# A slot of the load ring traded for a kept key tile, with projections done head by head, in a two-layer decode kernel

## Chip, cores, metric

One core of one Trainium2 chip. The metric is the device time of the kernel in microseconds (us), median of the runs of one kernel.

Names in this text: PE, DVE, ACT, POOL and SP are engines of the core. In this kernel PE does matmuls and transposes; DVE, ACT and POOL do the rest of the arithmetic and copy results; SP issues the loads. The DMA moves data from HBM, the large memory, into the core's own memory, where the kernel's tiles lie in 128 partitions; PE writes its results to PSUM. PE's "granted clock" is the share of full speed that the profile says it had. A load is "under way" from its issue by SP until all of it has landed. A run counts as slow when it is over 1.5% above the fastest run of its kernel.

Ratios and intervals are computed as the mean time of one kernel's fast runs over that of the other kernel's fast runs of the same rounds, so they are not quite the ratio of the medians that are quoted. Where a difference in us against the kernel before is given for an experiment ("-40 us"), it is the difference of the means of all fast runs of the two kernels in that set of runs.

## The reference, cut to what matters

```python
# B = 8 sequences, one new token each, D = 448, 16 query heads, 8 key/value heads,
# 4096 cached keys of 256 numbers (bf16); MLP width 1792
x = x + attention(layernorm(x), k_cache, v_cache, wq, wo)
y = layernorm(x)                        # with one token the block's mixer adds only zeros (w1, w2 drop out)
x = x + y + gelu(layernorm(y) @ w3) @ w4
# then both once more: a second layer with the SAME caches and weights
```

Both layers read the same key and value caches (134 MB each). A pass over keys and values for each layer would load all of it twice. The kernel keeps some transposed keys on the chip between the layers, so that layer 1 does not load and transpose them again.

## The kernel before

There are 8 batch elements, 8 key/value heads and 2 layers, so 128 "heads" of work in a fixed order `seq`. For each head, keys come in two half tiles of 1 MiB (2048 keys), values in two. All loads go through one ring of slots in this order; a slot is reused when PE has read it.

```python
N_RING = 5          # slots of 1 MiB (8 KB of each partition)
N_KEEP = 9          # kept half tiles of transposed keys, also 8 KB of each partition
CHAIN = 60
...
ring = [sb(f"ring{i}", [P, HALF, DH], bf) for i in range(N_RING)]
keep = [nc.alloc_sbuf_tensor(f"keep{i}", [P, HALF, P], f32) for i in range(N_KEEP)]
...
def kept(h, a):                       # half tile a of head h is kept for layer 1
    k = 2 * h + a
    return k if k < N_KEEP else None

def streamed(layer, h, a):            # is it loaded?
    return layer == 0 or kept(h, a) is None
...
def load_next():                      # the next chunk of the fixed order, into slot n % N_RING
    ...
    t, r = ring[n % N_RING]
    op("sp", lambda e: e.dma_start(t[:, :, :], src[b, h]...), writes=[r], dma=...)
```

One head of attention: PE transposes the keys in eight groups of four 128x128 blocks (`turn`), DVE or ACT copies each group from PSUM to SBUF, PE multiplies them with the queries (`score`), DVE/POOL/ACT make the softmax, and PE multiplies with the values of the head before (`pv`).

```python
ON_ACT = (1, 3, 5, 7)                 # of the eight groups of a head, those that ACT copies; DVE has the others
...
stream = any(streamed(layer, h, a) for a in range(2))
turns(0)
if stream and g > 1: finish(g - 2)
scores(0)
if stream: pv(g - 1, 0)
elif g > 1: finish(g - 2)
turns(1)
scores(1)
softmax(g)
if not stream: pv(g - 1, 0)           # a kept head frees two value slots one right after the other
pv(g - 1, 1)
```

Between the layers each batch element needs a **chain**: output projection, residual, norm, w3, GELU, w4, norm, query projection. The chain is a Python generator; `pump()`, called 14 times in a streamed head, puts its next steps into the instruction streams, as fast as a credit allows (a step with matmuls costs 1.0, one without 0.4). Before the first layer-1 head of the element, what is left of the chain is put in at once (`drain`).

```python
def mix(lo, n, then_q, project_out=True):
    for c in range(KC):
        for t in range(0, 32, 8):
            outputs(lo, n, c, range(t, t + 8), t == 0, True)      # 16 groups of 8 matmuls
            yield
    ...                                                           # norm, w3 (6 groups), gelu, w4 (8), norm
    yield from queries(lo, n)                                     # 16 groups, then one copy per half of the queries

def pump():
    credit["n"] = min(1.0, credit["n"] + credit["rate"]) if jobs else 0.0   # rate = CHAIN / (14*(per-1)) = 1.01
    while credit["n"] > 0.0:
        credit["n"] -= step()
...
if layer == 1 and all(s_[:2] != (1, b) for s_ in seq[:g]):
    drain()
```

In the order of heads, "kept" phases of ten heads (five layer-1 heads whose keys are kept, alternating with five layer-0 heads of the next element) alternate with "free" phases of five or six fully streamed heads. The chains run in the free phases.

Of the kernel before, what the change touches and what calls it, by code (L numbers as in the profile page):

```python
# [3 lines left out]
P = 128  # L4
B = 8
D = 448
HQ = 16
HKV = 8
# [10 lines left out]
GELU_K = 0.7978845608028654  # L19
RSQRT_MAGIC = 0x5F3759DF  # L20

N_RING = 5
N_KTR = 4
N_TK = 4
N_KEEP = 9
N_REP = 24
N_MLP = 24
CHAIN = 60
N_PS = 2


# [97 lines left out]
def decode_two_layers(nc, A_x, A_k_cache, A_v_cache, A_wq, A_wo, B_w3, B_w4, out):  # L129
# [42 lines left out]
    hw, r_hw = sb("hw", [P, NF, B], f32)  # L172
    hT, r_hT = sb("hT", [P, NF, B], bf)
    qT = nc.alloc_sbuf_tensor("qT", [P, B, 2, HQ], bf)
    r_q = [Res() for _ in range(B)]
    oT = nc.alloc_sbuf_tensor("oT", [P, HQ, 2, B], bf)
    r_o = [Res() for _ in range(B)]
    pT = [sb(f"pT{i}", [P, NI, 2], bf) for i in range(N_PS)]
# [15 lines left out]
    C_H = 32  # L194
    C_Q = 160
    C_L = 480


    op("pool", lambda e: e.memset(ident[:, :], 0.0), writes=[r_ident])
# [8 lines left out]
    op("dve", lambda e: e.memset(lnT[:, :, :], 0.0), writes=[r_ln, r_lift])  # L208

    op("dve", lambda e: e.memset(mm[64:P, C_Y:C_Y + B], 0.0), writes=[r_mm])  # L210


    full = N_KEEP // 2
# [155 lines left out]
    def kr(kc):  # L369
        return P if kc > 0 else 64  # L370
# [28 lines left out]
    def project(cols, r_w, at, ts, upper, n):  # L399

        def f(e):
            last = None
            for t in ts:
                for kc in (1, 2, 3, 0):
                    rhs = lnT[:, KC if kc == 0 and upper else kc, 0:n]
                    last = e.matmul(room(P, at + t * B, n), cols(kc, t), copies(rhs, n),  # L406
                                    start=(kc == 1), stop=(kc == 0), skip_group_check=True)
            return last
        op("pe", f, reads=r_w + [r_ln] + ([r_lift] if upper else []), writes=[r_mm])

    def queries(lo, n):

        yield from layernorm(lo, n, False)
        scaled(lnT, r_ln, 0, n)
        yield
        yield
        for t in range(0, 32, 2):
            project(wq_cols, wq_r, C_Q, range(t, t + 2), t >= 16, n)
            if t == 0:
                lift(n)  # L420
            yield
        for c in range(2):
            op("dve", lambda e, c=c: e.tensor_copy(  # L423
                qT[:, lo:lo + n, c, :],
                mm[:, C_Q:C_Q + 32 * B].rearrange("p (a c n) -> p n c a", n=B, c=2)[:, 0:n, c, :]),
               reads=[r_mm], writes=[r_q[b] for b in range(lo, lo + n)])

    def outputs(lo, n, c, ts, first, alone):

        def f(e):  # L430
            w = kr(c)
            last = None
            for t in ts:
                at = C_Y + c * B + lo
                cols = oT[:, t // 2, t % 2, lo:lo + n]
                last = e.matmul(room(w, at, n) if alone else mm[0:w, at:at + n], wo[:, t, row0(c):row0(c) + w],  # L436
                                copies(cols, n) if alone else cols, start=first and t == ts[0],
                                stop=False, skip_group_check=True)
            return last
        op("pe", f, reads=[r_wo] + [r_o[b] for b in range(lo, lo + n)], writes=[r_mm])  # L440

    def mix(lo, n, then_q, project_out=True):

        y_ = mm[:, C_Y:C_Y + KC * B].rearrange("p (c n) -> p c n", n=B)[:, :, lo:lo + n]
        x_ = xT[:, :, lo:lo + n]
        if project_out:
            for c in range(KC):
                for t in range(0, 32, 8):
                    outputs(lo, n, c, range(t, t + 8), t == 0, True)
                    yield  # L450
        op("dve", lambda e: e.tensor_tensor(x_, y_, x_, ALU.add), reads=[r_mm, r_x], writes=[r_x])
        yield from layernorm(lo, n, True)
        scaled(lnT, r_ln, 1, n)

# [23 lines left out]
           reads=[r_hb, r_hw], writes=[r_hT])  # L478
        yield
        for c in range(KC):  # L480
            for half in range(2):
                def f(e, c=c, half=half):
                    w = kr(c)
                    last = None
                    for t in range(7 * half, 7 * half + 7):
                        last = e.matmul(room(w, C_Y + c * B + lo, n), w4[:, t, row0(c):row0(c) + w],  # L486
                                        copies(hT[:, t, 0:n], n), start=(t == 0), stop=(t == NF - 1), skip_group_check=True)
                    return last
                op("pe", f, reads=[r_w4, r_hT], writes=[r_mm])
                yield  # L490
        op("dve", lambda e: e.scalar_tensor_tensor(x_, y_, 0.5, xres[:, :, 0:n], ALU.mult, ALU.add),
           reads=[r_mm, r_xres], writes=[r_x])
        yield
        if then_q:
            yield from queries(lo, n)

    jobs = []

    credit = {"n": 0.0, "rate": 1.0}

    def step():

        if jobs:
            n = len(S.ops["pe"])
            try:
                next(jobs[0])
            except StopIteration:
                jobs.pop(0)
            return 1.0 if len(S.ops["pe"]) > n else 0.4
        return 1.0  # L510

    def pump():
        credit["n"] = min(1.0, credit["n"] + credit["rate"]) if jobs else 0.0
        while credit["n"] > 0.0:
            credit["n"] -= step()

    def drain():
        while jobs:
            step()


# [26 lines left out]
    def attend(g):  # L548
# [41 lines left out]
        def score(f):  # L590
            kt, r_kt = kts[f]

            def fn(e):
                last = None
                for i in range(4):
                    at = C_S + 2 * (4 * f + i)
                    for c in range(2):

                        last = e.matmul(pst[:, at:at + 2 * N_REP].rearrange("p (r j) -> p r j", j=2), kt(i, c),  # L599
                                        repeated(qT[:, b, c, 2 * h:2 * h + 2]), start=(c == 0),  # L600
                                        stop=(c == 1), skip_group_check=True)
                return last
            op("pe", fn, reads=[r_kt, r_q[b]], writes=[r_ps])

        def turns(a):
            for f in range(4 * a, 4 * a + 4):
# [98 lines left out]
    for g, (layer, b, h) in enumerate(seq):  # L705
        last_of[layer, b] = g

    def all_but(h):

        ts = [t for t in range(32) if t // 4 != h]  # L710
        for c in (1, 2, 3, 0):
            for n in range(0, 28, 14):
                outputs(B - 1, 1, c, ts[n:n + 14], c == 1 and n == 0, False)
                yield

    def after(g):

        layer, b, h = seq[g]
        if g == len(seq) - 2:
            jobs.append(all_but(seq[-1][2]))  # L720
        if last_of[layer, b] != g:
            return
        if layer == 0:
            credit["rate"] = CHAIN / (14 * (per - 1))
            jobs.append(mix(b, 1, True))
        elif b == B - 2:
            jobs.append(mix(0, B - 1, False))
        elif b == B - 1:
            for c in range(KC):
                outputs(B - 1, 1, c, range(4 * h, 4 * h + 4), False, False)  # L730
            jobs.append(mix(B - 1, 1, False, False))

    jobs.append(queries(0, B))
    for g, (layer, b, h) in enumerate(seq):
        if layer == 1 and all(s_[:2] != (1, b) for s_ in seq[:g]):
            drain()
        w = attend(g)
        if g == 0:
            next(w)
            drain()  # L740
        for _ in w:
            pass
        if late:
            late.pop(0)()
# [76 lines left out]
```

## Time and profile before

| | before |
|---|---|
| time, median of 2 runs | 1261.01 us (1260.38 to 1261.63) |
| HBM read | 471.93 MB |
| DMA queue busy | 93.5% of 16 engines' span |
| PE busy | 77% |
| mean granted clock of PE | 0.885 |

The page of the kernel before: the rate in 40 equal slices of 31.6 us, and the loads' queue.

```profile
GB/s 316 378 415 420 374 322 398 420 404 295 384 419 419 371 335 421 419 419 355 358 421 419 378 307 418 421 419 308 399 420 420 401 319 421 420 414 295 362 312 122
...
q1 hardware_dynamic: 70496, 471.97, 93.5%
...
HBM read 471.93 MB, written 0.01 MB: 374 GB/s over the span
```

Rates of 419 to 421 GB/s are the best that occur, and they occur in many slices; about every 145 us a slice falls to 295 to 360. The part of the page on loads gives size and median time from issue to landing:

```profile
ring<-in_A_v_cache_dram SPq DMA_DIRECT2D x256, 1024.0 KB, 10.1
ring<-in_A_k_cache_dram SPq DMA_DIRECT2D x184, 1024.0 KB, 10.3
```

A load takes 2.5 us at 420 GB/s but 10 us from issue to landing: some four loads are under way at once.

Two stretches of the same trace (columns: from:to in us, their length, busy us and instructions of PE, of its weight loads, DVE, ACT and POOL, then PE's granted clock, mean DMA busy share, GB/s). The first is a kept phase, the second a chain:

```profile
340.00:400.00 60.00, 46.40 (x843) 40.89 (x840) 21.39 (x63) 15.83 (x46) 5.27 (x14) 0.89 1.01 420
700.00:747.00 47.00, 39.05 (x800) 34.64 (x800) 21.69 (x91) 10.91 (x29) 3.41 (x9) 0.85 0.90 341
```

In the first the DMA is the limit: 420 GB/s. In the second it moved 341 GB/s. What PE waited for, over the whole run (total us, number of waits, longest):

```profile
PE tk L575 <- DMA ring<-in_A_k_cache_dram: 124.1, 82, 2.7
...
PE mm L406 <- DVE lnT L365: 42.9, 10, 11.6
...
PE mm L406 <- DVE t L365: 31.3, 9, 5.0
...
PE mm L486 <- DVE hT L477: 10.1, 10, 1.5
```

L575 is a transpose of keys, L406 a projection (w3 or queries) and L486 one with w4; `lnT` and `t` are the two last DVE steps of a norm. The chain at 700 us shows what such a wait is (PE's instructions in time order: start, us, what, times; in brackets the idle time before and what ended it):

```profile
710.08 1.59 PE L575 MATMUL tk<-ident,ring 128*128 128x128 f32 x12 [0.15 <-DMA ring<-in_A_k_cache_dram]
714.89 0.26 PE L406 MATMUL mm<-lnT,w_sb 128*128 128x24 bf16 x3 [3.22 <-DVE t L365]
...
715.35 1.11 PE L575 MATMUL tk<-ident,ring 128*128 128x128 f32 x4
```

PE stands 3.22 us until the norm is done. Before the wait 12 transposes took 1.59 us, after it four take 1.11 us: half speed. The Trainium skill, page "TensorE: Matmul & The Clock Gate", Part 1, says PE's clock halves after an idle window of about 3.4 us and comes back after about as long a busy one; this trace agrees in kind (here a wait of 3.22 us was enough, and transposes were slow until about 720.8 us, some 6 us, with PE not busy all of that time).

### The profile page before, as it was taken

What the parts mean: (1) busy time and instruction counts of PE and PEld (TensorE: products, weight loads), DVE (VectorE), ACT (ScalarE), POOL (GpSimd) and SP (SyncE); (2) the same over time, 40 slices, a digit from 0 to 9 for tenths busy, and PEclk for the clock granted to TensorE, in tenths of its full rate; (3) what the DMA queues carried; (4) which work ended last, traced back from release to release, by engine and by line L of the source; (5) the groups of instructions that cost most, each with busy time, mean ns of one, the idle gap of its engine ahead of it and who ended that gap; (6) DMA issues with size and microseconds to landing.
All of it is one profiled execution on the core that took longest, in us unless ns stands there. A gap on an engine that the chain in (4) does not pass through costs nothing.

```text
span 1262.4 us, 42152 instructions
## 1 busy us (share of the span) xinstructions
PE 975.7 (77%) x19067; PEld 857.2 (68%) x19067; DVE 483.6 (38%) x1691; ACT 314.7 (25%) x891; POOL 104.9 (8%) x281
## 2 busy tenths in 40 slices
PE   2777887787886887877887888787777887787885
PEld 2666776676775776776776777676666776676774
DVE  2323442335333443335333443344333443334243
ACT  1223222222222222222222222231222222222120
POOL 0000000000000010000000000000100000000100
PEclk7879888888989989898889888897988988998886
DMA  8999989998999989999999989998999989998982
GB/s 316 378 415 420 374 322 398 420 404 295 384 419 419 371 335 421 419 419 355 358 421 419 378 307 418 421 419 308 399 420 420 401 319 421 420 414 295 362 312 122
DMA packets 70675, 474.66 MB, mean 376 GB/s; under 512 B 7248, under 2 KB 13280, under 8 KB 13792
## 3 DMA queue, kind: packets, MB, share of 16 engines
q1 hardware_dynamic: 70496, 471.97, 93.5%
q8 instruction: 149, 2.44, 0.8%
q14 instruction: 30, 0.25, 0.0%
HBM read 471.93 MB, written 0.01 MB: 374 GB/s over the span
## 4 chain that ended last, share of the span: by engine, by line
PE 44%; DMA 41%; DVE 9%; issue 4%; POOL 1%; SPq 1%; ACT 0%; POOLq 0%; ACTq 0%
DMA ring<-in_A_k_cache_dram 39%; PE tk L575 20%; PE ps L599 9%; PE pvb L673 5%; PE mm L406 4%; PE mm L436 2%; DMA ring<-in_A_v_cache_dram 2%; PE pvb L691 2%; DVE ktr L582 2%; PE mm L486 1%; SPq L269 1%; DVE sm L326 1%; DVE sm L327 1%; DVE sm L344 1%; DVE sm L325 1%
## 5 line engine op out<-in xcount | busy, mean ns | idle before, releaser
L575 PE MATMUL tk<-ident,ring 128*128 128x128 f32 x2944 | 459.3, 309 | 124.9 <-DMA ring<-in_A_k_cache_dram 124.1
L575 PEld LDWEIGHTS tk<-ident,ring 128*128 128x128 f32 x2944 | 370.1, 158 | 163.8 <-DMA ring<-in_A_k_cache_dram 153.5
L582 DVE COPY ktr<-tk 128x512 f32<-128x512 f32 x224 | 154.6, 690 | 244.8 <-PE tk L575 244.3
L580 ACT COPY ktr<-tk 128x512 f32<-128x512 f32 x224 | 131.2, 586 | 404.4 <-PE tk L575 404.4
L673 PE MATMUL pvb<-ring,pT 128*2 128x256 bf16 x4096 | 161.6, 279 | 47.8 <-DMA ring<-in_A_v_cache_dram 42.0
L582 DVE COPY keep<-tk 128x512 f32<-128x512 f32 x144 | 99.5, 691 | 170.2 <-PE tk L575 169.6
L599 PE MATMUL ps<-qT,keep 128*128 128x48 bf16 x4608 | 157.0, 187 | 5.6 <-DVE qT L423 3.6
L599 PEld LDWEIGHTS ps<-qT,keep 128*128 128x128 bf16 x4608 | 148.3, 99 | 17.7 <-issue 7.7
L580 ACT COPY keep<-tk 128x512 f32<-128x512 f32 x144 | 84.3, 586 | 266.3 <-PE tk L575 266.3
L655 ACT ACTIVATE pT<-ps,nb 128x32 bf16<-128x32 f32 x256 | 76.4, 298 | 252.3 <-DVE nb L651 234.7
L599 PE MATMUL ps<-qT,ktr 128*128 128x48 bf16 x3584 | 135.4, 188 | 0.6
L599 PEld LDWEIGHTS ps<-qT,ktr 128*128 128x128 bf16 x3584 | 122.5, 100 | 6.7 <-ACT ktr L580 1.5
L673 PEld LDWEIGHTS pvb<-ring,pT 128*2 128x2 bf16 x4096 | 76.0, 82 | 74.1 <-DMA ring<-in_A_v_cache_dram 47.3
L649 POOL PARTITION_ALL_REDUCE gm<-pm x128 | 45.4, 355 | 861.3 <-DVE pm L646 861.3
L406 PE MATMUL mm<-lnT,wq_sb 128*128 128x24 bf16 x864 | 48.0, 184 | 40.6 <-DVE lnT L365 40.3
L406 PEld LDWEIGHTS mm<-lnT,wq_sb 128*128 128x128 bf16 x864 | 43.3, 102 | 48.5 <-DVE lnT L365 42.4
L679 DVE COPY ob<-pvb 128x256 f32<-128x256 f32 x128 | 53.7, 420 | 51.1 <-PE pvb L673 50.5
L646 DVE TENSOR_REDUCE pm<-ps 128x2 f32<-128x64 f32 x128 | 28.7, 224 | 113.0 <-PE ps L599 113.0
L436 PE MATMUL mm<-oT,wo_sb 128*128 128x24 bf16 (+5 forms) x1280 | 61.5, 184 | 3.4 <-issue 2.2
L660 POOL PARTITION_ALL_REDUCE dn<-rs x128 | 51.1, 399 | 150.6 <-ACT pT L655 150.6
L691 PE MATMUL pvb<-ident,ob 128*128 128x128 f32 x256 | 58.4, 314 | 6.1 <-DVE ob L679 6.1
L436 PEld LDWEIGHTS mm<-oT,wo_sb 128*128 128x128 bf16 (+1 forms) x1280 | 52.1, 104 | 13.9 <-issue 10.1
(65 smaller groups left out, 477.4 us busy)
## 6 DMA issues: line engine op xcount, KB each, us to landing
ring<-in_A_v_cache_dram SPq DMA_DIRECT2D x256, 1024.0 KB, 10.1
ring<-in_A_k_cache_dram SPq DMA_DIRECT2D x184, 1024.0 KB, 10.3
wo_sb<-in_A_wo_dram SPq DMA_DIRECT2D x1, 3584.0 KB, 15.2
wq_sb<-in_A_wq_dram SPq DMA_DIRECT2D x3, 1024.0 KB, 11.2
w_sb<-in_B_w_dram SPq DMA_DIRECT2D x1, 1568.0 KB, 18.5
w_sb<-in_B_w_dram SPq DMA_DIRECT2D x3, 448.0 KB, 14.9
wqf_sb<-in_A_wq_dram SPq DMA_DIRECT2D x2, 256.0 KB, 14.8
w3f_sb<-in_B_w_dram SPq DMA_DIRECT2D x2, 112.0 KB, 15.8
```

The lines of the kernel that those rows point to most:

```text
L406: last = e.matmul(room(P, at + t * B, n), cols(kc, t), copies(rhs, n), start=(kc == 1), stop=(kc == 0), skip_group_check=True)
L436: last = e.matmul(room(w, at, n) if alone else mm[0:w, at:at + n], wo[:, t, row0(c):row0(c) + w], copies(cols, n) if alone else cols, star ...
L575: last = e.transpose(bank[:, j * P:(j + 1) * P], src[:, 4 * (f % 4) + j, :].bitcast(f32), ident4[:, :])
L580: op("act", lambda e: e.copy(flat, bank[:, :]), reads=[r_bank], writes=[r_kt])
L582: op("dve", lambda e: e.tensor_copy(flat, bank[:, :]), reads=[r_bank], writes=[r_kt])
L599: last = e.matmul(pst[:, at:at + 2 * N_REP].rearrange("p (r j) -> p r j", j=2), kt(i, c), repeated(qT[:, b, c, 2 * h:2 * h + 2]), start=(c ...
L649: op("pool", lambda e: e.partition_all_reduce(gm[q][0][:, :], pm[q][0][:, :], P, ReduceOp.max), reads=[pm[q][1]], writes=[gm[q][1]])
L655: return e.activation(pT[q][0][:, :, :].rearrange("p i j -> p j i")[:, j, :], pst[:, C_S:C_S + 2 * NI].rearrange("p (i j) -> p j i", j=2)[ ...
L660: op("pool", lambda e: e.partition_all_reduce(dn[q][0][:, :], rs[q][0][:, :], P, ReduceOp.add), reads=[rs[q][1]], writes=[dn[q][1]])
L673: last = e.matmul(pvb[at:at + 2, 0:DH], pT[q][0][:, a * HALF + i, :], v[:, i, :], start=(a == 0 and i < 4), stop=(a == 1 and i >= HALF - 4 ...
L679: op("dve", lambda e: e.tensor_copy(ob[:, :], pvb[:, 0:DH]), reads=[r_pv], writes=[r_ob])
L691: last = e.transpose(pvb[:, DH + c * P:DH + (c + 1) * P], ob[:, c * P:(c + 1) * P], ident4[:, :])
```

## The change

The intent: a fifth slot of the ring and a tenth kept half tile cost the same memory (8 KB of each partition). Trade the slot for the tile: eight loads of 1 MiB less. With that, the chain is lightened: the output projection of a head is done as soon as the head is done, the queries become usable head by head, and the chain runs at a slower pace of 0.6 step per pump.

```diff
-N_RING = 5
+N_RING = 4
-N_KEEP = 9
+N_KEEP = 10
-CHAIN = 60
+RATE = 0.6
@@ queries
+        for h in range(HKV):
+            for t in (4 * h, 4 * h + 2):
+                project(wq_cols, wq_r, C_Q, range(t, t + 2), t >= 16, n)
+                ...
+            op("dve", ... copy of this head's queries ..., reads=[r_mm], writes=[r_q[lo][h]])
+            ready[lo] = h + 1
+            yield
@@ output projection
+    def output(b, h):                 # 16 matmuls of one head, then xT += on DVE; a "side" job that goes first
+        ...
-        if project_out:               # no longer the first 16 groups of the chain
-            for c in range(KC): ...
@@ w4: one group of 14 matmuls for each c, not two of 7
@@ the end: outputs of the last element per head too, instead of 112 matmuls held for the end
@@ main loop
-        if layer == 1 and all(s_[:2] != (1, b) for s_ in seq[:g]):
-            drain()
+        while layer == 1 and ready[b] <= h:
+            step()
```

(The order of heads and loads is the same, except for the eight loads that fall away.)

More of the change, by code (lines that the diff above doesn't have):

```diff
@@ L174, in decode_two_layers @@
     qT = nc.alloc_sbuf_tensor("qT", [P, B, 2, HQ], bf)
-    r_q = [Res() for _ in range(B)]
+    r_q = [[Res() for _ in range(HKV)] for _ in range(B)]
     oT = nc.alloc_sbuf_tensor("oT", [P, HQ, 2, B], bf)
@@ L196, in decode_two_layers @@
     C_L = 480
+    C_P = 448
     op("pool", lambda e: e.memset(ident[:, :], 0.0), writes=[r_ident])
@@ L210, in decode_two_layers @@
     op("dve", lambda e: e.memset(mm[64:P, C_Y:C_Y + B], 0.0), writes=[r_mm])
+    op("dve", lambda e: e.memset(mm[64:P, C_P:C_P + 1], 0.0), writes=[r_mm])
     full = N_KEEP // 2
@@ L416, in queries @@
         yield
-        for t in range(0, 32, 2):
-            project(wq_cols, wq_r, C_Q, range(t, t + 2), t >= 16, n)
-            if t == 0:
-                lift(n)
+        for h in range(HKV):
+            for t in (4 * h, 4 * h + 2):
+                project(wq_cols, wq_r, C_Q, range(t, t + 2), t >= 16, n)
+                if t == 0:
+                    lift(n)
+                yield
+            if n > 1:
+                continue
+            op("dve", lambda e, h=h: e.tensor_copy(
+                qT[:, lo, :, 2 * h:2 * h + 2],
+                mm[:, C_Q + 4 * h * B:C_Q + 4 * (h + 1) * B].rearrange("p (a c n) -> p n c a", n=B, c=2)[:, 0, :, :]),
+               reads=[r_mm], writes=[r_q[lo][h]])
+            ready[lo] = h + 1
@@ L421, in queries @@
             yield
         for c in range(2):
-            op("dve", lambda e, c=c: e.tensor_copy(
-                qT[:, lo:lo + n, c, :],
-                mm[:, C_Q:C_Q + 32 * B].rearrange("p (a c n) -> p n c a", n=B, c=2)[:, 0:n, c, :]),
-               reads=[r_mm], writes=[r_q[b] for b in range(lo, lo + n)])
-    def outputs(lo, n, c, ts, first, alone):
+            if n > 1:
+                op("dve", lambda e, c=c: e.tensor_copy(
+                    qT[:, lo:lo + n, c, :],
+                    mm[:, C_Q:C_Q + 32 * B].rearrange("p (a c n) -> p n c a", n=B, c=2)[:, 0:n, c, :]),
+                   reads=[r_mm], writes=[r for b in range(lo, lo + n) for r in r_q[b]])
@@ L430, in f @@
+    def output(b, h):
         def f(e):
-            w = kr(c)
             last = None
-            for t in ts:
-                at = C_Y + c * B + lo
-                cols = oT[:, t // 2, t % 2, lo:lo + n]
-                last = e.matmul(room(w, at, n) if alone else mm[0:w, at:at + n], wo[:, t, row0(c):row0(c) + w],
-                                copies(cols, n) if alone else cols, start=first and t == ts[0],
-                                stop=False, skip_group_check=True)
-            return last
@@ L440, in outputs @@
-        op("pe", f, reads=[r_wo] + [r_o[b] for b in range(lo, lo + n)], writes=[r_mm])
-    def mix(lo, n, then_q, project_out=True):
+            for c in range(KC):
+                w = kr(c)
+                for t in range(4 * h, 4 * h + 4):
+                    last = e.matmul(room(w, C_P + c, 1), wo[:, t, row0(c):row0(c) + w],
+                                    copies(oT[:, t // 2, t % 2, b:b + 1], 1), start=(t == 4 * h),
+                                    stop=(t == 4 * h + 3), skip_group_check=True)
@@ new lines, in f, with outputs @@
+            return last
+        op("pe", f, reads=[r_wo, r_o[b]], writes=[r_mm])
+        yield
+        op("dve", lambda e: e.tensor_tensor(xT[:, :, b], mm[:, C_P:C_P + KC], xT[:, :, b], ALU.add),
+           reads=[r_mm, r_x], writes=[r_x])
+    def outputs(lo, n):
+        for c in range(KC):
+            def f(e, c=c):
+                w = kr(c)
+                last = None
+                for t in range(32):
+                    last = e.matmul(room(w, C_Y + c * B + lo, n), wo[:, t, row0(c):row0(c) + w],
+                                    copies(oT[:, t // 2, t % 2, lo:lo + n], n), start=(t == 0),
+                                    stop=(t == 31), skip_group_check=True)
+                return last
+            op("pe", f, reads=[r_wo] + [r_o[b] for b in range(lo, lo + n)], writes=[r_mm])
+            yield
+        y_ = mm[:, C_Y:C_Y + KC * B].rearrange("p (c n) -> p c n", n=B)[:, :, lo:lo + n]
+        op("dve", lambda e: e.tensor_tensor(xT[:, :, lo:lo + n], y_, xT[:, :, lo:lo + n], ALU.add),
+           reads=[r_mm, r_x], writes=[r_x])
@@ L444, in mix @@
+    def mix(lo, n):
         y_ = mm[:, C_Y:C_Y + KC * B].rearrange("p (c n) -> p c n", n=B)[:, :, lo:lo + n]
         x_ = xT[:, :, lo:lo + n]
-        if project_out:
-            for c in range(KC):
-                for t in range(0, 32, 8):
-                    outputs(lo, n, c, range(t, t + 8), t == 0, True)
-                    yield
-        op("dve", lambda e: e.tensor_tensor(x_, y_, x_, ALU.add), reads=[r_mm, r_x], writes=[r_x])
         yield from layernorm(lo, n, True)
@@ L480, in mix, with f @@
         for c in range(KC):
-            for half in range(2):
-                def f(e, c=c, half=half):
-                    w = kr(c)
-                    last = None
-                    for t in range(7 * half, 7 * half + 7):
-                        last = e.matmul(room(w, C_Y + c * B + lo, n), w4[:, t, row0(c):row0(c) + w],
-                                        copies(hT[:, t, 0:n], n), start=(t == 0), stop=(t == NF - 1), skip_group_check=True)
-                    return last
-                op("pe", f, reads=[r_w4, r_hT], writes=[r_mm])
-                yield
+            def f(e, c=c):
+                w = kr(c)
+                last = None
+                for t in range(NF):
+                    last = e.matmul(room(w, C_Y + c * B + lo, n), w4[:, t, row0(c):row0(c) + w],
+                                    copies(hT[:, t, 0:n], n), start=(t == 0), stop=(t == NF - 1), skip_group_check=True)
+                return last
+            op("pe", f, reads=[r_w4, r_hT], writes=[r_mm])
+            yield
         op("dve", lambda e: e.scalar_tensor_tensor(x_, y_, 0.5, xres[:, :, 0:n], ALU.mult, ALU.add),
@@ L493, in mix @@
         yield
-        if then_q:
-            yield from queries(lo, n)
-    jobs = []
-    credit = {"n": 0.0, "rate": 1.0}
+    jobs, side = [], []
+    ready = [0] * B
+    credit = {"n": 0.0}
     def step():
-        if jobs:
+        q = side or jobs
+        if q:
             n = len(S.ops["pe"])
             try:
-                next(jobs[0])
+                next(q[0])
             except StopIteration:
-                jobs.pop(0)
+                q.pop(0)
             return 1.0 if len(S.ops["pe"]) > n else 0.4
@@ L512, in pump @@
     def pump():
-        credit["n"] = min(1.0, credit["n"] + credit["rate"]) if jobs else 0.0
+        credit["n"] = min(1.0, credit["n"] + RATE) if jobs or side else 0.0
         while credit["n"] > 0.0:
@@ L517, in drain @@
     def drain():
-        while jobs:
+        while jobs or side:
             step()
@@ L602, in fn @@
                 return last
-            op("pe", fn, reads=[r_kt, r_q[b]], writes=[r_ps])
+            op("pe", fn, reads=[r_kt, r_q[b][h]], writes=[r_ps])
         def turns(a):
@@ L706, in decode_two_layers @@
         last_of[layer, b] = g
-    def all_but(h):
-        ts = [t for t in range(32) if t // 4 != h]
-        for c in (1, 2, 3, 0):
-            for n in range(0, 28, 14):
-                outputs(B - 1, 1, c, ts[n:n + 14], c == 1 and n == 0, False)
-                yield
     def after(g):
         layer, b, h = seq[g]
-        if g == len(seq) - 2:
-            jobs.append(all_but(seq[-1][2]))
+        if layer == 0 or b == B - 1:
+            side.append(output(b, h))
         if last_of[layer, b] != g:
@@ L723, in after @@
         if layer == 0:
-            credit["rate"] = CHAIN / (14 * (per - 1))
-            jobs.append(mix(b, 1, True))
+            jobs.extend([mix(b, 1), queries(b, 1)])
         elif b == B - 2:
-            jobs.append(mix(0, B - 1, False))
+            jobs.extend([outputs(0, B - 1), mix(0, B - 1)])
         elif b == B - 1:
-            for c in range(KC):
-                outputs(B - 1, 1, c, range(4 * h, 4 * h + 4), False, False)
-            jobs.append(mix(B - 1, 1, False, False))
+            jobs.append(mix(B - 1, 1))
     jobs.append(queries(0, B))
     for g, (layer, b, h) in enumerate(seq):
-        if layer == 1 and all(s_[:2] != (1, b) for s_ in seq[:g]):
-            drain()
+        while layer == 1 and ready[b] <= h:
+            step()
         w = attend(g)
```

## The prediction

> **What bounds the kernel now.** Mostly the DMA. The page has one queue busy 93.5% and 472 MB moved. In the table of stretches, undisturbed stretches run at 419 to 421 GB/s with PE waiting for key tiles (list of waits: 124 us for keys, 42 us for values). At 0.42 MB/us the bytes alone cost 1124 of the 1262 us. The DMA's shortfall against 421 GB/s, summed in 10 us stretches: about 11 us in the first 60 us, 9 to 14 us in each of eight places about 145 us apart (95 us in all), 8 us around 1200 to 1220, 20 us after the last load.
>
> The eight places are the chains between the layers (output projection, norm, MLP, norm, queries of one batch element), threaded through heads by a credit. There the chain of waits shows no DMA wait: PE paces. At 700 to 747 us, 14 half tiles (35 us of DMA) took 46.5 us. PE waits 3.2 and 3.6 us for the two layer norms (DVE and POOL steps in series), 0.9 us for GELU; 16 output groups cost 0.2 us each. After each long wait four transposes take 1.05 instead of 0.48 us for 6 to 8 us. The Trainium skill, "TensorE: Matmul & The Clock Gate", Part 1, says the clock falls to half after an idle window of about 3.4 us and returns after as much work; the trace agrees (0.26 against 0.12 us per transpose). So a wait costs about twice itself.
>
> **What the change does.**
> 1. Ten kept half tiles, not nine: 8 fewer 1 MiB loads, 463.6 MB. 8.39/0.42 = -20 us, all on the DMA path; also 128 fewer transposes (20 us PE). Head order unchanged.
> 2. Output projection per head (16 matmuls, 0.4 us, and a DVE add) where PE waits for DMA anyway: -3.3 us of PE per chain.
> 3. Credit 0.6 per pump, not about 1.0: in the changed instruction order about 5.5 us of PE work stand between the second norm's input and the first query matmul; the norm took 5.3 us. I expect the 3 us waits to fall to 0 to 1.5 us and most half-clock stretches in the chains to vanish.
> 4. Queries copied per head: the rest may run into the kept heads, where PE has slack. Added: 8 small copies per chain, each able to hold the next projection some tenths of a us.
> 5. Four ring slots: three loads in flight, 7.5 us of DMA work; a half tile is held at most 3.7 us. No loss in DMA-bound stretches, up to 2.5 us at a PE-bound place.
> 6. End: 100 output matmuls after the last head (3.9 us) become 16: -3 us.
>
> **Sum.** 463.6 MB at 0.42 = 1104; start 12; chains, about 12 of the 95 left; 1200 to 1220 region 6; tail 17; ring 6. Total 1157 us. Eight times in ten: 1142 to 1182. Chances: faster by over 2% 0.97, within 2% 0.02, slower 0.01.
>
> **What would show it.** Key loads 176; HBM read 463.5 MB; DMA busy about 96%; the low GB/s slices between 5 and 37 of 40 gone or above 390; PE waits on the norms inside the chains under 1.5 us; PE waits for DMA longer in spite of fewer loads.
>
> **What would make it wrong.** If four slots leave the DMA idle in steady stretches (below 415 GB/s), or many short waits of projections on DVE copies and adds replace the long ones, the chain places keep half their loss: about 1195. If nothing is left at the chains: 1145.

## The result

| | before | after |
|---|---|---|
| median | 1261.01 us | 1244.07 us (1242.79 to 1245.36) |
| ratio of fast runs | | 0.9866 (95%: 0.9817 to 0.9914) |
| HBM read | 471.93 MB | 463.54 MB |
| mean granted clock of PE | 0.885 | 0.898 |

The change is 17 us faster, not 104. The eight loads are gone as predicted, and they alone are 20 us of bytes. So everything else of the change together gained nothing, or lost a little. The page after:

```profile
GB/s 301 392 406 420 373 362 391 412 408 341 391 384 389 354 366 389 405 411 374 373 410 405 386 361 388 405 377 352 386 396 395 382 357 394 409 399 353 358 334 142
...
q1 hardware_dynamic: 69344, 463.58, 95.2%
...
HBM read 463.54 MB, written 0.01 MB: 374 GB/s over the span
...
ring<-in_A_v_cache_dram SPq DMA_DIRECT2D x256, 1024.0 KB, 8.2
ring<-in_A_k_cache_dram SPq DMA_DIRECT2D x176, 1024.0 KB, 7.8
```

The low slices did get shallower (341 to 374 instead of 295 to 360 through the middle of the run), but nearly all slices of 419 to 421 are gone too: 384 to 412 now. The DMA's *busy* share is higher than before (95.2%) at the same mean of 374 GB/s. Busy is not the same as fast. (The Trainium skill, "Perfetto Trace Analysis", section "Identifying the Most-Contended Engine", takes HBM utilization and not occupancy for the DMA; the two profile pages shown here agree.) A load now lands 8 us after its issue, not 10. Stretches, a kept phase and a chain:

```profile
340.00:400.00 60.00, 46.44 (x898) 40.54 (x896) 20.48 (x62) 15.36 (x46) 5.27 (x14) 0.89 0.98 385
684.00:746.00 62.00, 52.29 (x1047) 45.85 (x1047) 28.70 (x119) 15.55 (x42) 5.31 (x14) 0.92 0.97 373
```

The chain improved from 341 to 373 GB/s, its granted clock from 0.85 to 0.92; the kept phase, which has no chain in it and was at 420, fell to 385 at a busy share of 0.98. PE's waits after:

```profile
PE tk L598 <- DMA ring<-in_A_k_cache_dram: 136.2, 86, 5.6
...
PE ps L622 <- DVE ktr L605: 16.5, 13, 1.4
...
PE mm L408 <- DVE t L367: 15.2, 9, 5.0
...
PE mm L408 <- DVE lnT L367: 13.0, 9, 2.0
PE mm L408 <- DVE qT L427: 12.7, 25, 0.9
```

The waits on the norms fell from 42.9 + 31.3 us to 13.0 + 15.2 us. Two new ones stand beside them: scores that wait for DVE's copies of keys (16.5 us) and projections that wait for DVE's copies of queries (12.7 us).

To see the ring at work, PE in a kept phase of the changed kernel:

```profile
345.83 0.61 PE L696 MATMUL pvb<-ring,pT 128*2 128x256 bf16 x16 [1.19 <-DMA ring<-in_A_v_cache_dram]
348.32 3.67 PE L598 MATMUL tk<-ident,ring 128*128 128x128 f32 x16 [1.88 <-DMA ring<-in_A_k_cache_dram]
...
354.16 0.61 PE L696 MATMUL pvb<-ring,pT 128*2 128x256 bf16 x16
354.70 1.97 PE L598 MATMUL tk<-ident,ring 128*128 128x128 f32 x16
```

L696 reads a value slot, L598 a key slot. A slot becomes free at 346.4 (values) and the next only at about 352.0, when the key tile that landed at 348.3 has been transposed at half clock. SP issues loads at 346.5 and 352.1 us: for 5.5 us none can be issued, and the four loads that were under way run down to two. In the ring of five the same gap exists (issues at 340.1 and 345.6 us in the kernel before), but there it takes five loads down to three.

From issue and landing times of every load and the bytes that landed in each us, I worked out the rate by the number of loads under way (70 to 1170 us of the span):

```
loads under way          1        2        3        4        5
before   share of time   6%      16%      14%      45%      18%
         GB/s          216      345      389      417      418
after    share of time   1%      22%      57%      19%
         GB/s          296      355      391      413
```

Four loads under way carry the full rate, three about 390 and two about 350, in both kernels. The change moved most of the time from four or five to three. This is a correlation (few loads are also under way when PE is late), and the count alone doesn't fix the rate; the experiments below take the cause apart.

### The profile page after: what moved, and what is told of

It is laid out like the page before. It is cut to its first block, busy times and chain, and to the rows that moved or that the text cites. A ratio compares the mean times of both kernels' runs of the same rounds, so it can differ in the third digit from the quotient of the medians.

```text
span 1241.0 us, 41908 instructions
## 1 busy us (share of the span) xinstructions
PE 959.2 (77%) x18939; PEld 835.8 (67%) x18939; DVE 483.3 (39%) x1787; ACT 305.0 (25%) x875; POOL 104.8 (8%) x281
## 3 DMA queue, kind: packets, MB, share of 16 engines
q1 hardware_dynamic: 69344, 463.58, 95.2%
HBM read 463.54 MB, written 0.01 MB: 374 GB/s over the span
## 4 chain that ended last, share of the span: by engine, by line
PE 45%; DMA 40%; DVE 10%; issue 4%; POOL 0%; ACT 0%; SPq 0%; POOLq 0%; ACTq 0%
DMA ring<-in_A_k_cache_dram 40%; PE tk L598 22%; PE ps L622 8%; PE pvb L696 5%; PE mm L408 4%; DVE ktr L605 3%; PE mm L447 2%; PE pvb L714 2%; PE mm L510 1%; DVE sm L328 1%; DVE sm L329 1%; DMA ring<-in_A_v_cache_dram 1%; DVE sm L327 1%; DVE sm L346 1%; DVE xc L360 0%
## 5 line engine op out<-in xcount | busy, mean ns | idle before, releaser
L598 PE MATMUL tk<-ident,ring 128*128 128x128 f32 x2816 | 426.6, 308 | 143.8 <-DMA ring<-in_A_k_cache_dram 136.2
L598 PEld LDWEIGHTS tk<-ident,ring 128*128 128x128 f32 x2816 | 357.5, 158 | 186.6 <-DMA ring<-in_A_k_cache_dram 164.4
L605 DVE COPY ktr<-tk 128x512 f32<-128x512 f32 x192 | 132.4, 690 | 168.0 <-PE tk L598 167.7
L696 PE MATMUL pvb<-ring,pT 128*2 128x256 bf16 x4096 | 164.6, 282 | 42.3 <-DMA ring<-in_A_v_cache_dram 35.5
L605 DVE COPY keep<-tk 128x512 f32<-128x512 f32 x160 | 110.6, 691 | 196.1 <-PE tk L598 196.0
L622 PE MATMUL ps<-qT,keep 128*128 128x48 bf16 x5120 | 178.8, 185 | 4.4 <-issue 3.6
L603 ACT COPY ktr<-tk 128x512 f32<-128x512 f32 x192 | 112.3, 585 | 266.2 <-PE tk L598 266.1
L622 PEld LDWEIGHTS ps<-qT,keep 128*128 128x128 bf16 x5120 | 163.9, 98 | 18.3 <-issue 11.1
L696 PEld LDWEIGHTS pvb<-ring,pT 128*2 128x2 bf16 x4096 | 77.1, 83 | 70.1 <-DMA ring<-in_A_v_cache_dram 43.5
L622 PE MATMUL ps<-qT,ktr 128*128 128x48 bf16 x3072 | 109.1, 186 | 17.8 <-DVE ktr L605 16.5
L622 PEld LDWEIGHTS ps<-qT,ktr 128*128 128x128 bf16 x3072 | 100.6, 99 | 22.4 <-DVE ktr L605 19.2
L447 PE MATMUL mm<-oT,wo_sb 128*128 128x24 bf16 (+1 forms) x1152 | 53.5, 188 | 8.9 <-DVE oT L721 4.9
```

The costliest lines, as they stand in the source:

```text
L447: last = e.matmul(room(w, C_P + c, 1), wo[:, t, row0(c):row0(c) + w], copies(oT[:, t // 2, t % 2, b:b + 1], 1), start=(t == 4 * h), stop=( ...
L598: last = e.transpose(bank[:, j * P:(j + 1) * P], src[:, 4 * (f % 4) + j, :].bitcast(f32), ident4[:, :])
L603: op("act", lambda e: e.copy(flat, bank[:, :]), reads=[r_bank], writes=[r_kt])
L605: op("dve", lambda e: e.tensor_copy(flat, bank[:, :]), reads=[r_bank], writes=[r_kt])
L622: last = e.matmul(pst[:, at:at + 2 * N_REP].rearrange("p (r j) -> p r j", j=2), kt(i, c), repeated(qT[:, b, c, 2 * h:2 * h + 2]), start=(c ...
L696: last = e.matmul(pvb[at:at + 2, 0:DH], pT[q][0][:, a * HALF + i, :], v[:, i, :], start=(a == 0 and i < 4), stop=(a == 1 and i >= HALF - 4 ...
```

## The experiments

Fifteen more kernels ran, and all passed the comparison with the reference. Theory R (ring): four slots leave too few loads in flight, and that ate the gain of the schedule. Theory S (schedule): the chains never got cheaper, small waits replaced the long ones, and the ring is harmless. Names: b is the old schedule, a the new one, r the slots, k the kept half tiles.

| kernel | slots, kept | copies on ACT | pace | median us | ratio to before | difference of means, us |
|---|---|---|---|---|---|---|
| before | 5, 9 | 4 of 8 | 1.01 | 1261 | 1 | |
| after | 4, 10 | 4 of 8 | 0.6 | 1244.1 | 0.9866 | -17 |
| a_r5k9 | 5, 9 | 4 of 8 | 0.6 | 1219.1 | 0.969 | -39.9 |
| b_r4k9 | 4, 9 | 4 of 8 | 1.01 | 1309.2 | 1.0393 | +48.5 |
| a_r4k9 | 4, 9 | 4 of 8 | 0.6 | 1262.8 | 1.0026 | +3.4 |
| b_r4k10 | 4, 10 | 4 of 8 | 1.01 | 1290.9 | 1.0221 | +26.9 |
| a_r5k10w | 5, 10 | 4 of 8 | 0.6 | 1193.8 | 0.9443 | -69.0 |
| a_q8k10 | 8 quarter slots, 10 | 4 of 8 | 0.6 | 1216.5 | 0.9622 | -44.5 |
| a_r5k9_rate1 | 5, 9 | 4 of 8 | 1.0 | 1259.0 | 0.9966 | -3.0 |
| b_chain36 | 5, 9 | 4 of 8 | 0.6 | 1239.3 | 0.984 | -20.2 |
| b_act6 | 5, 9 | 6 of 8 | 1.01 | 1251.0 | 0.9933 | -8.5 |
| a_r5k9_act6 | 5, 9 | 6 of 8 | 0.6 | 1187.9 | 0.9417 | -72.3 |
| a_r5k9_act8 | 5, 9 | 8 of 8 | 0.6 | 1178.4 | 0.9352 | -81.4 |
| a_r5k9_act6_rate05 | 5, 9 | 6 of 8 | 0.5 | 1178.1 | 0.9353 | -81.6 |
| a_r4k10_act8 | 4, 10 | 8 of 8 | 0.6 | 1187.8 | 0.941 | -74.0 |
| a_r5k9_act8_rate05 | 5, 9 | 8 of 8 | 0.5 | 1174.9 | 0.9348 | -82.9 |
| a_r3k10 | 3, 10 | 4 of 8 | 0.6 | 1402.8 | 1.1154 | +144.1 |

The 95% intervals of these ratios reach 0.3 to 0.8% to either side, 3 to 10 us. "After", b_chain36 and b_act6 are less than 2% faster than the kernel before, though their intervals leave out 1; b_r4k10's interval straddles 2%. In b_r4k10 and a_r4k10_act8 one of four runs was slow: the median counts it, the last two columns do not.

### 1. The parts one by one: a_r5k9, b_r4k9, a_r4k9, b_r4k10

These four ran on one chip in one set, so their differences can be set against each other.

The new schedule with the old memory:

```diff
 # changed kernel
-N_RING = 4
+N_RING = 5
-N_KEEP = 10
+N_KEEP = 9
```

> The new schedule with the old memory (five slots, nine kept). Ring theory (four slots leave too few loads in flight, and that ate the gain of the schedule): DMA stretches outside the chains are back at 415 to 420 GB/s and the time is 1195 to 1220 us, below both kernels, although 8.4 MB more are loaded than after. Rival, schedule theory (the chains were never shortened; small waits on copies and adds took the place of the long ones): 1250 to 1265 us, about the kernel before, since the 20 us of bytes come back.

Measured: 1219.1 us, -40 us: faster than both kernels. The kept phase is back at full rate, the chain is where the changed kernel has it:

```profile
340.00:400.00 60.00, 44.86 (x870) 38.78 (x866) 23.75 (x78) 16.27 (x44) 4.94 (x13) 0.97 1.01 420
666.00:730.00 64.00, 54.98 (x1072) 48.06 (x1073) 29.09 (x120) 15.76 (x42) 4.94 (x13) 0.87 0.96 368
```

The old schedule with four slots, nothing else:

```diff
 # kernel before
-N_RING = 5
+N_RING = 4
```

> The kernel before with only its ring cut from five slots to four. Ring theory: the undisturbed stretches fall from 420 to about 385 to 400 GB/s and the time rises by 30 to 55 us, to 1290 to 1315 us. Schedule theory (the ring is harmless, as predicted blind): 1262 to 1275 us, with the undisturbed stretches still near 420 GB/s.

Measured: 1309.2 us, +48.5 us. A kept phase, at 420 GB/s in the kernel before, falls to 394 and lower:

```profile
350.00:410.00 60.00, 47.77 (x834) 41.95 (x834) 20.54 (x60) 15.32 (x44) 4.90 (x13) 0.85 0.98 394
500.00:560.00 60.00, 43.28 (x770) 37.20 (x774) 18.95 (x56) 13.96 (x41) 4.94 (x13) 0.83 0.97 381
```

The tenth kept tile alone, in the new schedule (the changed kernel with `N_KEEP = 9`):

> The new schedule with four slots and nine kept: beside the changed kernel it isolates the tenth kept half tile. If the 8 loads are worth their bytes: 1244 + 20 to 23 = 1262 to 1268 us under both theories. If below 1255 the kept tile is worth less than its bytes, because the stretch it left was not bound by bytes.

Measured: 1262.8 us, +3.4 us against before. The changed kernel stood at -17, so the tile is worth about 20 us (from runs on two chips, each against its own runs of before). The old schedule with four slots and ten kept (`N_RING = 4`, `N_KEEP = 10` in the kernel before):

> The old schedule with the new memory (four slots, ten kept). Ring theory: the memory trade alone costs about as much as it saves or more (ring +30 to 55, bytes -20): 1270 to 1295 us. Schedule theory: the memory trade is what gave the whole gain: 1240 to 1248 us, equal to the changed kernel.

Measured: 1290.9 us, +26.9 us. Against b_r4k9 the tile is worth 21.6 us.

In b_r4k9 the time with three loads under way, half of the run, ran at 393 GB/s, as it does in the changed kernel (its quarter with four at 396).

What follows: the ring is not harmless, so theory S is wrong there, and R holds (the small waits of theory S are real too: section 6). The new schedule is worth 40 us with five slots and 45 us with four. The lost slot costs 48.5 us in the old schedule and 43 us in the new one (3.4 + 39.9). The tile returns 20 to 22 with four slots. The sum -40 + 43 - 20 = -17 us is what the change measured, but it must be, since the three are steps between the same kernels; the check that does not follow of itself is that the old schedule gives nearly the same prices for slot and tile.

### 2. Slot and tile together: a_r5k10w

With both the fifth slot and the tenth tile the kernel does not build: the memory is short by some 7 KB of a partition. This kernel makes room by keeping only half of the output weights, a computation that is wrong.

```diff
 # changed kernel
-N_RING = 4
+N_RING = 5
-    wo, r_wo = sb("wo_sb", [P, 32, D], bf)
+    wo, r_wo = sb("wo_sb", [P, 16, D], bf)      # loaded twice, once with each half; t % 16 for t where it is read
```

> The changed kernel with five slots AND ten kept tiles, made to fit by keeping only half of the output weights (loaded twice into the same half, so that bytes, instructions and order stay; the result is wrong on purpose). If ring, bytes and schedule add up: 1219 - 20 = 1194 to 1204 us, which is 40 to 50 us below the changed kernel: the price of the fifth slot. If the fifth slot matters less once ten are kept: above 1215.

Measured: 1193.8 us, -69 us, so 52 us below the changed kernel's -17. The parts of section 1 add up to -60; the 9 us more are about what the noise of two such differences allows. So the effects add as far as these runs can tell, and the fifth slot is worth 43 to 52 us in every pair with half of the copies on ACT (section 7 has the other case). Against a_r5k9 the tile is worth 29 us here, not 20. (The comparison with the reference passed even so; presumably attention's share of the output is too small for its tolerance to notice. This kernel is a measurement, not a version.)

### 3. The same memory in smaller slots: a_q8k10

```diff
 # changed kernel; K and V chunks are quarter tiles, freed after 8 transposes or 8 value matmuls
-N_RING = 4
+N_RING = 8
-    ring = [sb(f"ring{i}", [P, HALF, DH], bf) for i in range(N_RING)]
+    ring = [sb(f"ring{i}", [P, QUART, DH], bf) for i in range(N_RING)]      # QUART = NI // 4; further lines cut
```

> The changed kernel with the same ring memory cut into eight slots of quarter tiles (512 KB loads), ten kept. A slot is then free after 8 transposes and not 16, so about half a half-tile more is in flight. If the bytes in flight are what counts: 1215 to 1236 us and more stretches above 410 GB/s. If it were the number of half tiles of lead (bytes of ring) alone, or if smaller descriptors cost rate: 1240 us or more.

Measured: 1216.5 us, -44.5 us: 27 us better than the changed kernel with not a byte of memory more. So the bytes of ring alone do not set the time; how soon a slot can be loaded again counts too. By my count of issues and landings 3.1 MiB were under way on average, against 2.9 MiB in the changed kernel. It pays a price, though: no slice of its page is above 410. The best it does,

```profile
600.00:660.00 60.00, 47.20 (x952) 38.29 (x949) 21.02 (x69) 15.42 (x48) 6.02 (x16) 0.94 1.03 409
```

is 409 GB/s, at a DMA busy share of 1.03: loads of 512 KB with rows of 4 KB run about 3% slower than those of 1 MiB with 8 KB. Which of the two, the size of the load or of the row, was not separated.

### 4. A dose: a_r3k10

```diff
 # changed kernel
-N_RING = 4
+N_RING = 3
```

> The changed kernel with three slots, ten kept: a dose for the loads in flight. From the rates found for one and two loads in flight in the traces (about 330 and 385 GB/s, against 412 to 420 for three and four), with mostly one to two in flight: 340 to 365 GB/s through the steady stretches and 463.6 MB, so 1330 to 1420 us. If four slots lost for another reason (the trade of a slot with its neighbours, the order of loads) and the number in flight did not matter: below 1280 us.

Measured: 1402.8 us. Over 300 us in the middle of the run:

```profile
400.00:700.00 300.00, 219.92 (x4028) 192.12 (x4023) 104.90 (x384) 66.73 (x192) 22.79 (x61) 0.86 0.90 337
```

337 GB/s, slightly less than I expected. In the count of loads under way, 58% of the time has two, at 339 GB/s, and 28% three, at 369. (The expectation's rates for one to three loads are not those of the table above. They come out of the same traces if a load counts only until the first of its 16 completions: 286 to 318, 390 to 397 and 412 to 416 GB/s.) Slots of 5, 4, 3 give, with the new schedule and ten kept tiles, 1194 (a_r5k10w), 1244, 1403 us: the loss grows fast below five.

### 5. What the schedule gave: a_r5k9_rate1, b_chain36

The schedule gave 40 us where the prediction had put over 80. Which part of it gave them? The new schedule at the old pace:

```diff
 # a_r5k9
-RATE = 0.6
+RATE = 1.0
```

> Five slots, nine kept, new schedule, but credit 1.0 per pump as before instead of 0.6. If the spreading is what shortened the waits on the norms: the waits of projections on DVE grow by 15 us or more and the time is 1228 to 1242 us. If moving the output projection out of the chain did it: 1215 to 1224 us.

Measured: 1259.0 us, -3 us, with 3 us inside the noise. All of the schedule's gain is gone although the output projection is still out of the chain. The waits on the norms are those of the kernel before again (it had 42.9 and 31.3):

```profile
PE mm L408 <- DVE lnT L367: 44.2, 10, 10.4
...
PE mm L408 <- DVE t L367: 24.0, 9, 5.0
```

The pace alone, in the kernel before:

```diff
 # kernel before
-CHAIN = 60
+CHAIN = 36
```

> The kernel before (five slots, nine kept) with the pace of its chains alone cut from 1.0 to 0.6 of a step per pump. The whole chain then does not fit before the first layer-1 head and what is left is emitted in one run. If the pace alone is what won 40 us: 1220 to 1230 us. If the pace only pays because the outputs were taken out of the chain and the queries may run past the first layer-1 head: 1262 us or more, up to 1300, with long runs of projections between heads.

Measured: 1239.3 us, -20 us: between the two expectations. Pace alone gives half. I put the other half down to the room for the slow chain that the early outputs and the head-by-head queries make; no run takes these two apart. Together they gave nothing clear of noise at pace 1.0.

### 6. What held the chains after that: a_r5k9_act6, b_act6, a_r5k9_act8, a_r5k9_act6_rate05

PE in a chain of a_r5k9:

```profile
696.87 0.56 PE L622 MATMUL ps<-qT,ktr 128*128 128x48 bf16 x16
698.64 0.57 PE L622 MATMUL ps<-qT,ktr 128*128 128x48 bf16 x16 [1.21 <-DVE ktr L605]
700.47 0.26 PE L408 MATMUL mm<-lnT,wq_sb 128*128 128x24 bf16 x3 [1.25 <-DVE lnT L367]
...
701.88 1.11 PE L598 MATMUL tk<-ident,ring 128*128 128x128 f32 x4
```

The single wait of over 3 us has become two of 1.2 us: first the scores wait for a copy of keys by DVE, then the projection for the norm. Both are work of DVE, which takes its instructions in the order of the program (the 1787 of the changed kernel stand in the trace in that order, but for one pair at the start; ACT's 618 stand so too). So the norm's small steps (about 0.17 us each, some 25 of them) and the key copies (0.69 us each) delay one another: here the copy that the scores waited for began at 697.90 us, behind steps of the norm that ran from 697.32. And the transposes after it are at half speed again (1.11 us for four). ACT was busy 26% of the time. So move copies to ACT (0.586 us each there):

```diff
 # a_r5k9
-    ON_ACT = (1, 3, 5, 7)
+    ON_ACT = (1, 2, 3, 5, 6, 7)
```

> Five slots, nine kept, new schedule, with six of eight key copies on ACT and two on DVE instead of four and four. Theory for the part of the chain loss that stayed: the norm's 25 small DVE steps and the key copies share one in-order queue, so scores wait for their key copies (15 us in total) and projections for the norm (35 us). Then this takes most of the 15 us away and shortens the norm: 1200 to 1213 us. Rival, PE is simply full in the chains (its own work and its half clock): 1216 to 1225, no change; or ACT becomes the new late one and it is slower.

Measured: 1187.9 us, -72.3 us, so 32 us better than a_r5k9, and twice the waits that I had counted: the waits seem to cost more than themselves. The waits of scores on key copies are gone from the list. The waits on the norms did not shrink: they are 27.7 and 20.4 us, after 19.7 and 15.2 in a_r5k9.

All waits of PE for DVE between 60 us and 25 us before the end tell more than the norms alone (my sums over the traces): 74.7 us in the kernel before, 73.2 in a_r5k9, 51.3 here. The new schedule with five slots won its 40 us with the same sum of waits; what changed is that 17 waits of over 2 us (57.5 us) became 3 (10.1 us) and many short ones.

The same edit, six copies on ACT, in the kernel before:

> The kernel before with six of eight key copies on ACT. If the DVE queue alone held the chains: it gains as it did in the new schedule, 31 us, to about 1230 us. If the norm's serial steps hold the chain at pace 1.0 whatever the copies do: waits on the norms stay above 50 us and the time is 1245 to 1260 us.

Measured: 1251.0 us, -8.5 us: a quarter. At pace 1.0 waits of 37.7 and 30.6 us on the norms stay, so there the norm's serial steps hold the chain. All eight copies on ACT:

```diff
 # a_r5k9_act6
-    ON_ACT = (1, 2, 3, 5, 6, 7)
+    ON_ACT = (0, 1, 2, 3, 4, 5, 6, 7)
```

> The same at pace 0.6 with all eight key copies on ACT. ACT then has about 5.3 us of work for each head of 10 us. If only DVE's queue matters: 1178 to 1188 us. If the exponentials, which stand in the same in-order queue and wait for DVE and POOL, hold the key copies up: 1195 us or more, with waits of PE on ACT copies.

Measured: 1178.4 us, -81.4 us. The exponentials on ACT do not get in the way, and PE's waits for DVE, summed as above, are 17.3 us. Six copies and pace 0.5 (`RATE = 0.5`):

> Best version so far (five slots, nine kept, new schedule, six copies on ACT: 1188 us) at pace 0.5. If the waits on the norms that stay (some 35 us in total beside start and end) shrink further: 1176 to 1185 us. If the chain now runs too late for the first layer-1 head and is bunched there: 1190 to 1205 us.

Measured: 1178.1 us, the same (33.6 us of such waits, none over 2 us).

### 7. Ring or late copies, and the best version: a_r4k10_act8, a_r5k9_act8_rate05

With four slots, late copies could also be part of the ring's price, since a stalled PE frees slots late. The changed kernel with all copies on ACT:

> The changed kernel with all key copies on ACT. With five slots that took 41 us. If the four slots lose rate because of loads in flight alone, the steady stretches stay below 410 GB/s and the time stays 20 us or more above the five-slot version with the same copies (1178): 1198 to 1215 us. If they lost because late key copies and norm waits held slots too long, most of the loss goes: 1160 to 1180 us, and the ten kept tiles win after all.

Measured: 1187.8 us (mean of its three fast runs 1183.7, one run was slow), -74 us: between the two. It gained 57 us, against 41.5 with five slots. If the tile is worth 20 us here too, four slots and nine kept would stand at -54, and the slot's price falls from 43 to about 27 us; with the 29 us that the tile was worth at five slots it is 36 (estimates from these numbers, with the noise of several sets of runs in them). So some of the price of the slot was probably PE's own lateness, and more than half of it stays. Lateness did shrink: 29% of key loads lay in their slot for over 3.7 us from landing to the end of the last transpose in the changed kernel, 7% here. And three loads under way, 72% of the time, carry 404 GB/s here, not 391: the count of loads does not fix the rate. In its kept phases:

```profile
470.00:530.00 60.00, 45.57 (x918) 39.22 (x915) 9.01 (x46) 23.85 (x64) 5.50 (x15) 0.94 1.00 397
600.00:660.00 60.00, 48.31 (x962) 42.03 (x959) 9.30 (x48) 24.46 (x66) 5.27 (x14) 0.91 1.01 412
```

The last two gains together, five slots, nine kept, all copies on ACT, pace 0.5:

> Five slots, nine kept, all key copies on ACT, pace 0.5: the two last gains together. If both took away the same waits: 1172 to 1179 us, no more than either. If they add: 1165 to 1171 us. The floor of bytes at 420 GB/s, start and end is about 1155 us.

Measured: 1174.9 us, -82.9 us, ratio 0.9348 (0.9322 to 0.9373). They overlap nearly whole: each alone had cut the waits on the norms between start and end from 34 us to 5 to 7 us. It is the best version that ran. The waits on the norms that remain are those at the start and at the end:

```profile
PE tk L598 <- DMA ring<-in_A_k_cache_dram: 140.0, 124, 2.4
...
PE mm L408 <- DVE lnT L367: 8.7, 2, 8.4
...
PE mm L408 <- DVE t L367: 5.1, 1, 5.1
...
PE mm L408 <- DVE qT L427: 2.2, 4, 0.9
```

and its slices have no dips left from the third to the last but one (lowest 390):

```profile
GB/s 362 388 415 421 415 419 417 416 419 404 418 417 409 418 420 417 410 420 391 421 417 419 406 420 418 406 421 415 418 412 419 412 411 415 419 420 403 414 390 115
```

## Why the prediction was wrong, point by point

1. *"Ten kept half tiles ... -20 us"*: right. 463.54 MB were read (463.5 predicted); the tile measured 20 to 22 us with four slots (29 with five).
2. *"Output projection per head ... -3.3 us of PE per chain"*: the work moved as said, but it bought no time by itself: at pace 1.0 the new schedule is equal to the old one within noise (a_r5k9_rate1). What it may give is room for the slower pace.
3. *"I expect the 3 us waits to fall to 0 to 1.5 us"*: right on the waits. (13.0 + 15.2 - 5.0 us, leaving out the one of 5 us at the end, over 17 waits is 1.4 us each.) **Wrong on what followed**, *"most half-clock stretches in the chains to vanish"* and *"chains, about 12 of the 95 left"*: the schedule saved 40 us, not some 83, and of the transposes 20% still ran at the slow pace (over 180 ns from start to start), after 21% before. I had taken the DVE work of the norm as a fixed 5.3 us beside PE's, and forgot that DVE also copies half of the keys PE needs, in the same queue. The wait on the norm became a wait on key copies, 16.5 us in total where the kernel before had next to none, and PE still fell to half clock. Taking the copies away gave 32 to 41 us more. The prediction had named this sign as well (*"many short waits of projections on DVE copies and adds replace the long ones"*), but put the time at about 1195 us if either came true; both did.
4. *"8 small copies per chain, each able to hold the next projection some tenths of a us"*: right (25 waits, 12.7 us, so 0.5 us each), but left out of the sum.
5. *"Four ring slots: ... No loss in DMA-bound stretches, up to 2.5 us at a PE-bound place"*, "ring 6" in the sum: **this is the other step that failed, and the one that the experiments isolate best.** The slot cost 43 us in this schedule (48.5 in the old one), and by the stretches shown mostly where I expected none (kept phase 385 GB/s against 420 in a_r5k9, chain 373 against 368). The argument was that three loads under way are 7.5 us of DMA work and no tile is held longer than 3.7 us. Both halves were wrong. Tiles are held longer: from landing to the last read, 29% of the key loads and 25% of the value loads of the changed kernel took over 3.7 us, up to 7.0. And slots are not freed evenly (5.5 us between two releases in the kept phase, because two value slots are freed 1.8 us apart and the next key tile has still to land and be transposed at half clock), while three loads under way did not carry 420 GB/s here but 391. I took the mean rate of a full queue to hold for any queue that is not empty. The failure sign I had named was a right one: *"If four slots leave the DMA idle in steady stretches (below 415 GB/s)"*; they did, at 385, though its busy share still read 0.98.
6. *"End: ... -3 us"*: right. From the end of the last value matmul to the end of the run it was 19.5 us before and is 16.5 after.

Of the 87 us between prediction and result, about 37 are the ring (43 against 6) and about 46 the chains (the schedule's 40 us hold the 3 of the end, so 37 saved against 83); the last 4 are not accounted for, and are within the noise.

What stays open: why two or three loads of 1 MiB under way do not fill 16 DMA engines. The trace has a hint: the 16 completions of one load are spread over 2.7 us (median, before) from the first engine to the last, longer than a load takes at the full rate. The Trainium skill, "DMA: Bandwidth & Descriptors", section "Queues, rings and completion order", says each engine has its own ring for a queue, and its section "Two DMAs through the same engine are not ordered" says that nothing orders transfers across engines. So engines that are ahead would run out of work first when little is queued. That fits, but no run here isolates it.

## What to carry to other kernels

Before trading a buffer of a load ring for anything, count the loads under way in the trace and look at the gaps between the releases of slots, not at the mean hold time; a ring needs to cover the longest gap and still leave enough queued for the full rate, and a high busy share does not show that it does. When a chain of small dependent steps is spread out to hide its latency, look at what else stands in the queue of the same engine: the wait may only change its name. Smaller slots of the same total memory gave back 27 us of a missing slot here, at a price of some 3% in rate.

## What the Trainium skill lacked or had wrong

- "DMA: Bandwidth & Descriptors", section "Bandwidth", gives rates by the size of one transfer (341 GB/s for 1 MB, 425 for 16 MB, for DMAs issued from GpSimd), and no page says how many transfers have to be under way for the full rate. Here, issued from SP, 1 MiB loads: about 350 GB/s with two, 390 with three and 413 to 417 with four under way in the kernels before and after (three carried 369 to 404 in other runs, so the count is not the whole rule), and 1194, 1244 and 1403 us for rings of five, four and three slots.
- The same section says that for transfers from HBM to SBUF "the HBM side (~358) binds", in a sentence without the condition that its own note gives (both cores of the pair loading). The one core that this program uses held 420 GB/s over 60 us here, near the page's own 425 GB/s for one core.
- "Perfetto Trace Analysis" warns that the DMA's occupancy misleads, but has no case of it: here the busy share stayed near 1 while the rate fell, 385 GB/s at 0.98 against 420 GB/s at 1.01.
